# One core, windowed attention with a gated side branch: w_out goes to the head of the main load queue, w_in behind it

## The chip, the cores and the metric

The kernel runs on one core of a Trainium2 chip. A core has five engines that run side by side: TensorE (PE, matrix products), VectorE (DVE), ScalarE (ACT), GpSimd (POOL) and SyncE (SP), and 16 DMA engines that bring data from the chip's main memory into the on-chip memory of 128 partitions. In this kernel SP does little but issue loads; all loads that it issues stand in one queue. The metric is the device time of one execution in microseconds (us); lower is better. All data are 32-bit floats.

## The reference

Two sequences (B = 2), one new token each, width D = 512. The token's row is normalised, and goes two ways. One is attention over the last 4096 positions of a cache of 32768, with 32 query heads that share 8 key and value heads (4 to 1) of 128 numbers each. The other is a small gated network whose result, through SiLU, multiplies what attention gives.

```
xn = layernorm(x)                                    # (2, 1, 512)

# attention
q = xn @ wq                                          # wq (512, 4096): 32 heads of 128
k, v = last 4096 positions of the caches             # 8 heads, each used by 4 query heads
p = softmax(q k^T / sqrt(128))
s = (p v) @ wo                                       # wo (4096, 512)

# gate
z  = gelu(xn @ w_in)                                 # w_in (512, 1792)
z1, z2 = two halves of z (896 each);  z2 = layernorm(z2)
h  = z1 * (w_sp * z2 + b_sp)                         # w_sp, b_sp: one number each, as there is one token
g  = silu(h @ w_out)                                 # w_out (896, 512)

out = x + s * g
```

Most bytes are the keys and values: 2 x 2 x 8 x 4096 x 128 numbers, 67 MB. wq and wo have 8.4 MB each, w_in 3.67 MB and w_out 1.84 MB.

## The kernel before, in words

**Buffers.** Big loads land in a pool `ring` of four slots (up to 32 KB in each partition), which are used again in turn: `win` takes the first, `wq0` and `wq2` (two loads into its halves) the next two, the first keys `k0` the fourth; `k1` takes win's slot when the matmuls on win are through, `v0` that of `wq0`, `k2` that of `wq2`, `v1` that of `k0`, and so on. A second pool, `kts`, has two buffers. They hold `wout` and `z` first, then `qs` and `qx` (the queries on their way into another layout), then the transposed keys. The vector engine's transpose into `qx` waits for the matmuls that read `wout`, since `qx` takes its buffer.

**Order.** Every instruction of TensorE, VectorE, ScalarE and SP keeps the order in which the program is written (the class `InOrder`, so that nearly every instruction has the line 65 in the profile). Each engine works through its own list and waits at an instruction until its operands and buffers are ready. SP's list is: `win`, `wout`, three loads for w_q, then the keys and values in pairs of heads (eight units of 4.19 MB of keys and as much of values), and wo last. Completions of DMAs are counted on a few lanes that are used in turn; a load that takes a lane again waits until the lane's load before it has landed. The first load on SP's list and the first load of keys have the same lane.

**Front of the kernel (lines 118 to 339).** While `win` comes in, x is normalised and turned into columns (`xnT`), and constant tables are made. Then TensorE has, in this order: `z` (xn times w_in, in four pieces; ScalarE and VectorE copy the results out), `zT` (28 small matmuls that turn z into columns), `queries(0)`, a mean, `queries(1)`, a variance, `queries(2)`, `queries(3)` (16 matmul instructions each, on the four row blocks of w_q), and `y`, the product of the gate's hidden row `hT` with `wout`. VectorE and ScalarE work on GELU, the second layer norm and `hT` at the same time. `hT` is made from zT, the mean and the variance. Behind y come `qx` (transposed queries), `xm`, the matmul `qa`, and `y_sum`.

**The units (ORDER, line 27).** A string lists the steps of the attention part in the order in which they are issued. For unit 0 the list starts with the loads `K:0 K:1 V:0`, then `T:0.0` (the first of eight transposes of the unit's keys on VectorE, `kts<-k`), `q:0` (VectorE places the queries, `qb`), more transposes, and then `shares` and `scores` (TensorE), row maxima, exponentials (ScalarE, `p`), their transposes (`pT`), and `pv` (TensorE, `acc`, 16 instructions each for two halves). Later units have the same steps, one unit interleaved with the next. At the end come the products with wo (`part`, `so`), the sum with x and the store.

Of the kernel before, what the change touches and what calls it, by code (L numbers as in the profile page):

```python
# [9 lines left out]
F32 = mybir.dt.float32  # L10
# [4 lines left out]
P = 128  # L15
# [55 lines left out]
def kernel(  # L71
# [14 lines left out]
    pe, dve, act, sp = (InOrder(tc, e) for e in (nc.tensor, nc.vector, nc.scalar, nc.sync))  # L86
    B, _, D = x.shape
# [9 lines left out]
    FT = FH // P  # L97
# [8 lines left out]
    kts = ctx.enter_context(tc.tile_pool(name="kts", bufs=2))  # L106
# [4 lines left out]
    def slot(name, *shape):  # L111
        return ring.tile([P, *shape], F32, tag="slot", name=name)
# [5 lines left out]
    xs = sb.tile([B, D], F32, tag="ss", name="xs", bufs=1)  # L118
    act.dma_start(xs, x[:, 0, :])
    win_v = w_in.rearrange("(p k) f -> p k f", p=P)  # L120
    win = slot("win", KT, F)
    sp.dma_start(win, win_v)
    wout = kts.tile([P, FT, D], F32, tag="kts", name="wout")
    sp.dma_start(wout, w_out.rearrange("(p j) d -> p j d", p=P))
    wq_v = wq.rearrange("(p k) f -> p k f", p=P)
    wqt = []
    for a in range(0, KT, 2):
# [475 lines left out]
    for u in range(NU):  # L603
        p = Unit()
        p.u, p.m, p.kt, p.sh, p.ss, p.s, p.p, p.pT = u, None, {}, {}, {}, {}, {}, {}
        units.append(p)
    for line in ORDER.strip().split("\n"):
        for name in line.split():
            name, at = name.split(":")
# [35 lines left out]
```

## Time and profile before

| what | value |
|---|---|
| time, median of 3 runs | 216.86 us (216.77 to 216.94) |
| the profiled execution's own time | 217.29 us |
| its span, first to last instruction | 215.5 us |
| outside the span | 1.79 us |
| mean granted TensorE clock | 0.825 of full |
| busy: TensorE, VectorE, ScalarE, GpSimd | 143.2, 126.7, 51.6, 4.5 us |
| read from memory | 89.40 MB, 415 GB/s over the span |

The views used further on are these. The page's rows by slices cut the span into 40 equal parts and give tenths. A view by stage gives, for a stretch of time, the busy time of each engine with the number of its instructions, the granted clock, the mean busy share of the 16 DMA engines and the rate. A share slightly over 1 comes from packets that are counted where they begin. A timeline row gives the start, the length, the engine, the operation with its tiles, and in brackets how long the engine was idle before and what ended that. The chain that ended last goes back from the last instruction to whatever released each step. The list of DMA issues gives the size in KB and the time from issue to landing. PE is TensorE, PEld its loading of weights, SPq the queue of instructions that SP issues. A tile's view gives its instructions with least, median and greatest length in nanoseconds, and first and last start.

### The profile page before, as it was taken

Reading aid. Unit: us, or ns where it says so; the run is one execution under the profiler, and the core shown is the slowest. Engines: PE = TensorE matmul, PEld = TensorE weight load, DVE = VectorE, ACT = ScalarE, POOL = GpSimd, SP = SyncE. Lnnn points to the kernel's source line nnn. Section 1 sums busy time; section 2 is a strip of 40 time slices with the busy share of each in tenths; the row PEclk is TensorE's granted clock in tenths of the full one; section 3 lists DMA queues with packets and bytes.
Section 4 is the critical chain, followed back from the end, with each engine's and each line's share of the span. In section 5 each row is a group of like instructions: output and inputs, shape, how many; then the busy total and the mean of one; then the engine's idle time right before and its main releaser. Section 6 shows DMA issues by size and latency. Waiting matters only on the chain.

```text
span 215.5 us, 2332 instructions
## 1 busy us (share of the span) xinstructions
PE 143.2 (66%) x900; PEld 48.1 (22%) x900; DVE 126.7 (59%) x218; ACT 51.6 (24%) x129; POOL 4.5 (2%) x17
## 2 busy tenths in 40 slices
PE   0179796833854966964991795389259917987793
PEld 0117622111120221222220231123112201232231
DVE  2611213169899799649928972993698099636011
ACT  5011103300116036033330602142051206142201
POOL 8000000000000000000000000000000000000000
PEclk9999569665998896796697599669755997996999
DMA  7999999999999999999999999999999999999990
GB/s 246 432 443 444 398 429 465 414 458 414 456 408 447 420 426 444 426 443 426 450 420 450 408 441 420 426 450 426 447 415 456 401 456 414 447 426 417 420 374 22
DMA packets 3930, 89.54 MB, mean 416 GB/s; under 512 B 446, under 2 KB 462, under 8 KB 848
## 3 DMA queue, kind: packets, MB, share of 16 engines
q1 hardware_dynamic: 3900, 89.40, 96.8%
q8 instruction: 7, 0.11, 0.2%
q14 instruction: 3, 0.02, 0.0%
q10 hardware_dynamic: 20, 0.01, 0.0%
HBM read 89.40 MB, written 0.00 MB: 415 GB/s over the span
## 4 chain that ended last, share of the span: by engine, by line
DMA 63%; PE 23%; DVE 8%; ACT 3%; issue 1%; ACTq 0%
DMA v<-in_A_v_cache_dram 42%; DMA k<-in_A_k_cache_dram 16%; PE acc L65 10%; DMA win<-in_B_w_in_dram 5%; PE sh L65 5%; DVE kts L65 4%; PE part L65 4%; PE s L65 3%; DVE pT L65 1%; ACT p L65 1%; ACT o L65 1%; DVE gate L65 1%; PE mo L65 1%; ACT ss L65 1%; DVE qb L65 1%
## 5 line engine op out<-in xcount | busy, mean ns | idle before, releaser
L65 DVE STREAM_TRANSPOSE kts<-k 128x1024 f32<-128x1024 f32 x64 | 75.6, 1218 | 29.5 <-DMA k<-in_A_k_cache_dram 29.5
L65 PE MATMUL sh<-kts,qb 128*32 128x512 f32 x256 | 41.6, 775 | 13.2 <-DVE kts L65 9.3
L65 PE MATMUL acc<-v,pT 128*32 128x512 f32 x256 | 37.4, 707 | 8.8 <-DVE pT L65 4.4
L65 ACT ACTIVATE p<-s,nb 128x512 f32<-128x512 f32 x32 | 22.5, 733 | 36.2 <-DVE nb L65 36.2
L65 ACT ACTIVATE ss<-sh 128x512 f32<-128x512 f32 x16 | 9.6, 599 | 59.1 <-PE sh L65 59.1
L65 DVE STREAM_TRANSPOSE pT<-p 128x1024 f32<-128x1024 f32 x16 | 19.6, 1225 | 2.3 <-ACT p L65 2.1
L65 PE MATMUL s<-ss,sums 128*128 128x512 f32 x32 | 18.8, 671 | 2.3 <-ACT ss L65 2.3
L65 PE MATMUL mo<-mg,joint 128*128 128x16 f32 x16 | 4.0, 327 | 23.4 <-DVE mg L65 23.4
L65 PEld LDWEIGHTS acc<-v,pT 128*32 128x32 f32 x256 | 10.5, 145 | 35.1 <-issue 27.0
L65 PEld LDWEIGHTS sh<-kts,qb 128*32 128x32 f32 x256 | 8.8, 126 | 34.2 <-issue 28.8
L65 DVE TENSOR_REDUCE m<-s 128x1 f32<-128x512 f32 x16 | 10.7, 671 | 4.2 <-PE s L65 4.2
L65 PE MATMUL q_ps<-wq,xnT 128*32 128x512 f32 x64 | 10.5, 784 | 3.5 <-DMA wq<-in_A_wq_dram 3.5
L65 ACT ACTIVATE o<-acc,wd 128x128 f32<-128x128 f32 x32 | 9.1, 368 | 15.0 <-PE acc L65 15.0
L65 PEld LDWEIGHTS mo<-mg,joint 128*128 128x128 f32 x16 | 3.2, 250 | 27.2 <-DVE mg L65 24.4
L65 PE MATMUL z<-win,xnT 128*32 128x448 f32 x32 | 5.6, 869 | 4.7 <-DMA win<-in_B_w_in_dram 4.7
L65 PE MATMUL part<-wo,oT 128*32 128x512 f32 x56 | 7.7, 596 | 1.4 <-ACT o L65 1.4
L65 PEld LDWEIGHTS s<-ss,sums 128*128 128x128 f32 x32 | 5.0, 197 | 10.3 <-issue 7.7
L65 PE MATMUL zT_ps<-rowm,z 128*128 128x2 f32 x28 | 6.6, 370 | 0.0
L65 PEld LDWEIGHTS zT_ps<-rowm,z 128*128 128x128 f32 x28 | 6.5, 325 | 0.0
L65 ACT ACTIVATION_READ_ACCUMULATOR p<-s,nb 128x1 f32 x32 | 6.5, 203 | 0.0
L65 ACT ACT_TABLE_LOAD x4 | 5.1, 1283 | 2.6 <-POOL hT L164 2.6
L65 DVE COPY z<-z 128x448 f32<-128x448 f32 x2 | 1.3, 626 | 7.5 <-PE z L65 7.5
(111 smaller groups left out, 68.4 us busy)
## 6 DMA issues: line engine op xcount, KB each, us to landing
k<-in_A_k_cache_dram SPq DMA_DIRECT2D x8, 4096.0 KB, 27.4
v<-in_A_v_cache_dram SPq DMA_DIRECT2D x8, 4096.0 KB, 29.8
wq<-in_A_wq_dram SPq DMA_DIRECT2D x1, 4096.0 KB, 24.5
wq<-in_A_wq_dram SPq DMA_DIRECT2D x2, 2048.0 KB
wo<-in_A_wo_dram SPq DMA_DIRECT2D x1, 4096.0 KB, 30.4
win<-in_B_w_in_dram SPq DMA_DIRECT2D x1, 3584.0 KB, 11.5
wo<-in_A_wo_dram SPq DMA_DIRECT2D x1, 2048.0 KB
wout<-in_B_w_out_dram SPq DMA_DIRECT2D x1, 1792.0 KB, 15.3
```

Of the source, the lines that this page charges most:

```text
L65: return self.tc.keep_in_program_order(call(*args, **kwargs))
```

## The change

The two tiles are made and the two loads are issued in the other order. The pools are different (`ring` and `kts`), and each pool sees its own tiles in the same order as before, so that every tile keeps its place. On TensorE, VectorE, ScalarE and GpSimd the lists of instructions stay as they are. On SP the first two entries change places, and with them the lanes: the one that the first load of keys uses again belongs to `wout` afterwards, and to `win` before.

```
     win_v = w_in.rearrange("(p k) f -> p k f", p=P)
+    wout = kts.tile([P, FT, D], F32, tag="kts", name="wout")
+    sp.dma_start(wout, w_out.rearrange("(p j) d -> p j d", p=P))
     win = slot("win", KT, F)
     sp.dma_start(win, win_v)
-    wout = kts.tile([P, FT, D], F32, tag="kts", name="wout")
-    sp.dma_start(wout, w_out.rearrange("(p j) d -> p j d", p=P))
     wq_v = wq.rearrange("(p k) f -> p k f", p=P)
```

## The prediction

> **What bounds the kernel now.** I read the page first (span, DMA row, clock row, queues), then DMA share and rate by stage, then the timeline of the first 50 us by engine, then the chain that ended last and the last output-weight loads. The page's rows: the DMA row gives the mean busy share of the 16 DMA engines in 40 slices of 5.4 us, the PEclk row the granted TensorE clock in the same slices.
>
> ```profile
> span 215.5 us, 2332 instructions
> ...
> PEclk9999569665998896796697599669755997996999
> DMA  7999999999999999999999999999999999999990
> ...
> q1 hardware_dynamic: 3900, 89.40, 96.8%
> ```
>
> The main queue's DMAs (q1) carry 89.40 MB and keep the DMA engines busy for 96.8% of the span. By stage (window, its length, busy time of PE, PEld, DVE, ACT, POOL, and at the end of each row granted clock, DMA share, GB/s):
>
> ```profile
> 0.00:2.00 2.00, 0.00 (x0) 0.00 (x0) 0.35 (x2) 0.00 (x0) 1.45 (x12) 1.00 0.82 203
> 2.00:4.00 2.00, 0.00 (x0) 0.00 (x0) 1.15 (x5) 1.42 (x2) 2.00 (x4) 1.00 0.58 229
> ...
> 14.00:44.00 30.00, 24.51 (x140) 11.08 (x131) 7.08 (x28) 6.08 (x10) 0.00 (x0) 0.77 1.01 435
> 44.00:200.00 156.00, 106.04 (x642) 32.00 (x646) 113.52 (x159) 40.87 (x110) 0.00 (x0) 0.80 1.00 432
> ...
> 209.00:212.00 3.00, 2.90 (x52) 1.24 (x48) 0.00 (x0) 0.60 (x1) 0.00 (x0) 1.00 0.36 137
> ```
>
> From 14 to 200 us the engines are full (share 1.01 and 1.00, 435 and 432 GB/s); at that rate 89.40 MB alone take about 206 us. There is a start-up loss in the first 4 us and a run-out after 209. Two views of the end of the kernel, the tile wo (which instruction, how often, durations, first and last start) and the chain that ended last (start, length, what):
>
> ```profile
> L65 SPq DMA_DIRECT2D wo<-in_A_wo_dram x6: 334/426/432, 171.6 to 186.0; - x6
> ...
> DMA to landing us min/median/max: 25.5/25.7/30.4
> ```
> ```profile
> 77.09 27.29 DMA v<-in_A_v_cache_dram
> ...
> 195.29 3.27 PE acc L65 x16
> ...
> 198.87 1.93 PE acc L65 x16
> ...
> 211.33 0.93 PE so L65 x24
> ```
>
> The last load of wo is issued at 186.0 and lands 25.5 later, at 211.5. The last output matmuls (so) run from 211.33 to 212.26 and use it. The chain names PE in those last microseconds, but stream and TensorE arrive together there. So the time is the length of one unbroken stream of loads plus a short tail. The question for this change is whether the stream starts later, gets a hole, or moves other bytes.
>
> **The change, step by step.** It removes and adds nothing: the same two loads, 3.67 MB (128 rows of 28,672 bytes) and 1.84 MB (128 rows of 14,336), both on SP's queue, swap places. Instruction order on PE, DVE, ACT and POOL is the same. SP, and how the two loads land now:
>
> ```profile
> 0.73 0.39 SPq L65 DMA_DIRECT2D win<-in_B_w_in_dram  x1
> ...
> 1.18 0.41 SPq L65 DMA_DIRECT2D wout<-in_B_w_out_dram  x1
> ...
> 12.23 6.27 SPq L65 DMA_DIRECT2D k<-in_A_k_cache_dram  x2
> ...
> 32.50 0.53 SPq L65 DMA_DIRECT2D v<-in_A_v_cache_dram  x1
> ...
> 39.53 0.54 SPq L65 DMA_DIRECT2D k<-in_A_k_cache_dram  x1
> ```
> ```profile
> win<-in_B_w_in_dram SPq DMA_DIRECT2D x1, 3584.0 KB, 11.5
> ...
> wout<-in_B_w_out_dram SPq DMA_DIRECT2D x1, 1792.0 KB, 15.3
> ```
>
> *Landing times.* win lands at 0.73 + 11.5 = 12.2, wout at 1.18 + 15.3 = 16.5. Whatever is second lands when both are in, so win moves to about 16.5: 4.3 us later. wout lands first: its share is 4.3 us of transfer, and the start-up is 11.5 - 2 x 4.3 = 2.9, so near 0.7 + 7.2 = 7.9, where nobody needs it yet. Everything behind the pair (w_q, K, V) has the same bytes ahead of it: 0.
>
> *SP's queue.* The wait ahead of the first K load is a completion lane that this load shares with the first load of the queue; the row of SP's waits shows it:
>
> ```profile
> SPq L65 <- DMA win<-in_B_w_in_dram: 8.8, 1, 8.8
> ```
>
> After the swap that lane belongs to wout, so K0 is issued near 7.9, not 12.23. It stands behind w_q in the queue either way: 0. K1 needs win's buffer back, which is when the z matmuls end, near 18.0 now (the second issue, half a microsecond long, at the end of the row of 6.27 us) and near 22.3 after. The queue ahead of it is not empty before K0 has landed, just before 46.17 (the first key transpose, below): 23 us of cover. V0 (32.50) and K2 (39.53) wait for the query matmuls, dealt with next.
>
> *The front chain.* This is the only work that really moves. PE, in order (start, length, what, idle before it):
>
> ```profile
> 12.35 5.56 PE L65 MATMUL z<-win,xnT 128*32 128x448 f32 x32 [4.73 <-DMA win<-in_B_w_in_dram]
> ...
> 18.15 6.60 PE L65 MATMUL zT_ps<-rowm,z 128*128 128x2 f32 x28
> 26.18 3.64 PE L65 MATMUL q_ps<-wq,xnT 128*32 128x512 f32 x16 [1.43 <-DMA wq<-in_A_wq_dram]
> ...
> 30.29 2.14 PE L65 MATMUL q_ps<-wq,xnT 128*32 128x512 f32 x16
> 32.36 0.39 PE L65 MATMUL var_ps<-u,ones 128*128 128x14 f32 x2
> 32.68 1.92 PE L65 MATMUL q_ps<-wq,xnT 128*32 128x512 f32 x16
> 36.69 2.79 PE L65 MATMUL q_ps<-wq,xnT 128*32 128x512 f32 x16 [2.09 <-DMA wq<-in_A_wq_dram]
> 39.24 2.79 PE L65 MATMUL y<-wout,hT 128*32 128x512 f32 x14
> 44.27 1.12 PE L65 MATMUL qa<-xm,same 128*128 128x256 f32 x2 [2.25 <-DVE xm L65]
> ```
> ```profile
> 36.28 0.18 DVE L65 TENSOR_TENSOR hT<-zT 128x14 f32<-128x14 f32 x1
> ...
> 42.15 1.30 DVE L65 STREAM_TRANSPOSE qx<-qs 128x512 f32<-128x512 f32 x2 [5.68 <-PE y L65]
> ...
> 46.17 1.25 DVE L65 STREAM_TRANSPOSE kts<-k 128x1024 f32<-128x1024 f32 x1 [2.05 <-DMA k<-in_A_k_cache_dram]
> 47.34 1.19 DVE L65 TENSOR_TENSOR qb<-qa,grpm 128x1024 f32<-128x1024 f32 x1
> ```
>
> z starts near 16.65 and zT ends at 24.75 + 4.3 = 29.05. The first query group then finds its weights landed and loses its idle 1.43, so it starts at 29.05, 2.87 late. From there to the end of the third group PE runs without a break, 26.18 to 34.60, which now ends at 37.47. The fourth group, which waits 2.09 for w_q until 36.69 today, starts at 37.47: only 0.78 late. hT (36.46 + 2.87 = 39.33) is ready before PE is through with that group, so y ends at 42.03 + 0.78 = 42.81. Behind y come qx, the matmul qa and the placed queries qb. The qa matmul would end at 45.39 + 0.78 = 46.17, and qb starts at 47.34 because DVE first waits for K0 (2.05 idle). Cover: about 1.95; cost 0.
>
> Bounds: the same 16 query matmuls took between 1.92 and 3.64. All slow: the second, third and fourth groups add 1.50, 1.72 and 0.85, and y ends 4.9 late, 2.9 beyond the cover. All fast: y ends earlier than now, gain hidden. I take 0.78, because it leaves each row its own length. Without the cover those 2.9 us, or the 0.78, would fall on unit 0 first. What is late next is its V buffer, and the next covers are DVE's waits for later K loads:
>
> ```profile
> 75.42 3.50 DVE L65 STREAM_TRANSPOSE kts<-k 128x1024 f32<-128x1024 f32 x3 [1.41 <-DMA k<-in_A_k_cache_dram]
> ...
> 94.75 3.50 DVE L65 STREAM_TRANSPOSE kts<-k 128x1024 f32<-128x1024 f32 x3 [3.89 <-DMA k<-in_A_k_cache_dram]
> ```
>
> 1.41 and 3.89 us, 5.3 together, take up either. Nor would the queue run dry: the V load issued at 77.09 lands 27.29 later, while its own 4.19 MB need 9.7 at 432 GB/s, so some 17 us of other loads stand ahead of it.
>
> The Trainium skill, "TensorE: Matmul & The Clock Gate", Part 1 (the HAM clock gate), says that TensorE runs at half clock after an idle window of some 3.4 us and gets the full clock back after a busy one, in windows that run free of the kernel. The PEclk row (5 and 6 in the fifth and sixth slices, around the tiny zT matmuls and the first query group) agrees. By that rule, with the idle 2.09 gone, y would more often be warm and the front chain would end no later than today; by the rows it ends 0.78 late. Under the cover both give 0.
>
> *Start-up.* The first rows of the stream are now half as long; no row here shows a start with such rows. In the first 4 us the queue moved 203 x 2 + 229 x 2 = 0.86 MB against 1.74 MB at 435 GB/s: 2.0 us lost, part of it before the first byte. If the loss is a fixed time, the price is 0. If the start is paced per row (0.86 MB is 30 rows of 28,672), half-length rows move 0.43 MB less in that time: +1.0. If the loss per first row goes with its length, half of about 1 us is gained: -0.5. I take 0, nearest to what the two windows show: both are slow, and the rate is full afterwards with whichever rows.
>
> *Sum:* 217.29 of the profiled execution (215.5 of span and 1.79 around it) + 0 = 217.3; on the median of the runs, 216.86, which is 0.43 lower, it gives 216.9.
>
> **Rivals.**
>
> *Row-paced start (slower).* Place: the first 4 us of the stream. Price 0.5 (only the first row of each engine: 16 x 14,336 bytes = 0.23 MB) to 1.0, hence 217.4 to 217.9. For it: the rate in 2 to 4 us is still half. Against: once running, the stream holds 435 GB/s through wout's short rows as well. It decides if 0.19 MB or more are missing by 4 us. 0.15.
>
> *Length-paced start (faster).* 216.86 - 0.5 = 216.4, by the same windows. It needs the first rows' delay to shrink with their length. 0.08.
>
> *The tail's clock.* The 16 pv matmuls at 195.29 took 3.27, the same 16 at 198.87 took 1.93. If the half-clock stretch falls elsewhere, the tail shrinks or grows by about 1.3: 215.6 or 218.2. Against the gain: the last wo lands at 211.5 whatever PE does. Against both: units start on K landings by then, which do not move. 0.02 faster, 0.04 slower. The page of the Trainium skill named above has those windows run free of the kernel, so that the stretch would not hang on this change; no trace here shows their start.
>
> *The front delay reaches the end (slower).* It needs the queue to run dry, that is 17 us of cover used up by 4.9 at most; it would add at most 2.9: 219.8. 0.02.
>
> *The swap does nothing at all to landings,* because both loads interleave on the engines: against it stand 12.2 and 16.5. The time is the same, so it is within the forecast.
>
> **How the numbers follow.** Forecast, no change beyond 0.2% (0.43 us, about what a measurement of this kernel can tell from none): 0.69. Faster 0.08 + 0.02 = 0.10, and 0.02 more for what I have not seen: 0.12. Slower 0.15 + 0.04 + 0.02 = 0.21, of which the lower edge of the row-paced start may still be within the bound: 0.19. Range: 216.4 (the gain at start-up) to 217.6 (the row-paced start up to its middle); outside are the upper half of that rival, the tail and the front delay.
>
> **What would show it.** win's landing near 15.8 us after its issue and z at 16.6 show the first step; K0's issue near 8 the second. PE without idle between the zT matmuls and y, and y's end between 41 and 44, show the chain; DVE's first key transpose still at 46.2 the cover; share and rate of 14:44 and 44:200 unchanged, the unbroken stream; wo's last landing at 211.5 the end. Wrong would be: a rate well off 864 KB in the first 4 us (a start-up rival), a first key transpose that no longer waits for K0 and later K waits that shrink (front delay), or a DMA share under 0.98 in 14:200 (a hole in the stream).

## The result and the profile after

The changed kernel took 217.19 us (median of 20 runs, 217.00 to 217.36), the kernel before 216.83 in the same session (20 runs, 216.60 to 217.08). The ratio is 1.0016, with a 95% interval of 1.0009 to 1.0023: 0.36 us more, inside the 0.2% of the forecast, but not nothing. The profiled execution of after took 217.18 us with a span of 215.4. That of before, 217.29 with 215.5, lies above all 20 later runs of its kernel. So the two profiles differ in the opposite direction to the medians, and the 0.36 us cannot be found by laying these two side by side.

What the change did to the order of things can be. These are the main queue's issues and the landing times in the kernel after:

```profile
0.73 0.38 SPq L65 DMA_DIRECT2D wout<-in_B_w_out_dram  x1
1.18 0.41 SPq L65 DMA_DIRECT2D win<-in_B_w_in_dram  x1
...
8.05 14.10 SPq L65 DMA_DIRECT2D k<-in_A_k_cache_dram  x2
34.92 0.54 SPq L65 DMA_DIRECT2D v<-in_A_v_cache_dram  x1
38.81 0.54 SPq L65 DMA_DIRECT2D k<-in_A_k_cache_dram  x1
```
```profile
win<-in_B_w_in_dram SPq DMA_DIRECT2D x1, 3584.0 KB, 15.3
...
wout<-in_B_w_out_dram SPq DMA_DIRECT2D x1, 1792.0 KB, 7.3
```

win lands at 1.18 + 15.3 = 16.5, exactly when wout landed before; wout at 8.0, and K0 is issued then. TensorE and VectorE in the front, and VectorE's later waits for keys, in the kernel after:

```profile
16.65 4.91 PE L65 MATMUL z<-win,xnT 128*32 128x448 f32 x32 [9.03 <-DMA win<-in_B_w_in_dram]
...
21.79 6.60 PE L65 MATMUL zT_ps<-rowm,z 128*128 128x2 f32 x28
28.32 3.64 PE L65 MATMUL q_ps<-wq,xnT 128*32 128x512 f32 x16
...
35.10 3.64 PE L65 MATMUL q_ps<-wq,xnT 128*32 128x512 f32 x32
39.14 1.92 PE L65 MATMUL y<-wout,hT 128*32 128x512 f32 x14 [0.40 <-DVE hT L65]
```
```profile
46.44 1.25 DVE L65 STREAM_TRANSPOSE kts<-k 128x1024 f32<-128x1024 f32 x1 [3.29 <-DMA k<-in_A_k_cache_dram]
...
95.12 3.50 DVE L65 STREAM_TRANSPOSE kts<-k 128x1024 f32<-128x1024 f32 x3 [3.83 <-DMA k<-in_A_k_cache_dram]
```

z starts 4.30 us later than before (12.35), but y is done at 41.06, 0.97 us earlier than before (42.03). VectorE now waits 3.29 us for K0 instead of 2.05. The front was shortened on its way: the last two query groups (32 instructions in 3.64) and y (1.92 instead of 2.79) ran at the higher clock, without the idle 2.09 that stood between the groups before (granted clock from 14 to 44 us: 0.88, against 0.77 before).

The stream, by stage, in the kernel after (the same columns as in the prediction), and one row of before that was not shown there:

```profile
0.00:2.00 2.00, 0.00 (x0) 0.00 (x0) 0.35 (x2) 0.00 (x0) 1.45 (x12) 1.00 0.39 81
2.00:4.00 2.00, 0.00 (x0) 0.00 (x0) 1.16 (x5) 1.43 (x2) 2.00 (x4) 1.00 0.73 244
4.00:14.00 10.00, 0.61 (x4) 0.55 (x4) 3.28 (x22) 1.54 (x3) 1.01 (x4) 1.00 1.02 438
14.00:44.00 30.00, 24.72 (x146) 11.64 (x146) 7.21 (x28) 6.08 (x10) 0.00 (x0) 0.88 1.01 434
44.00:200.00 156.00, 103.82 (x637) 31.67 (x640) 113.27 (x158) 40.83 (x110) 0.00 (x0) 0.80 1.00 432
```
```profile
4.00:14.00 10.00, 2.26 (x16) 1.19 (x20) 3.27 (x22) 1.55 (x3) 1.01 (x4) 1.00 0.96 412
```

There is no hole in it: share 1.01 and 1.00 as before. The first 4 us look worse (81 x 2 + 244 x 2 = 650 KB against 864), while by 14 us the changed kernel looks ahead (0.65 + 4.38 = 5.03 MB after, 0.86 + 4.12 = 4.98 before). Neither can be read that way. The view books a whole packet (one row of a load) where it begins, so what it shows depends on how long the rows are that are in flight at the window's edge: at 4 us they are short in the kernel after, at 14 us in the kernel before. With the bytes of each packet spread evenly over its time, the four profiles of the old order (before twice, and two experiments below) have 4.86 to 4.90 MB at 14 us and 11.78 to 11.82 at 30, the three of the changed kernel 4.80 to 4.83 and 11.72 to 11.75. On average 0.05 MB are missing, 0.12 us at 432 GB/s, and at 199 us the same 0.05 MB are still missing (84.69 to 84.72 against 84.63 to 84.67). So about a third of the 0.36 us is lost by the whole stream in its first 14 us.

### The profile page after: what moved, and what is told of

Same layout as the page of the kernel before. It is cut to its first block, busy times and chain, and to the rows that moved or that the text cites. A ratio compares the mean times of both kernels' runs of the same rounds, so it can differ in the third digit from the quotient of the medians.

```text
span 215.4 us, 2332 instructions
## 1 busy us (share of the span) xinstructions
PE 140.5 (65%) x900; PEld 47.9 (22%) x900; DVE 126.7 (59%) x218; ACT 51.6 (24%) x129; POOL 4.5 (2%) x17
## 4 chain that ended last, share of the span: by engine, by line
DMA 60%; PE 18%; DVE 16%; ACT 3%; issue 1%; ACTq 0%
DMA k<-in_A_k_cache_dram 42%; DMA wo<-in_A_wo_dram 15%; DVE kts L65 11%; PE sh L65 7%; PE acc L65 4%; PE part L65 4%; DMA wout<-in_B_w_out_dram 3%; PE s L65 3%; ACT p L65 2%; DVE pT L65 2%; DVE m L65 1%; ACT ss L65 1%; DVE gate L65 1%; DVE nb L65 1%; DVE qb L65 1%
## 5 line engine op out<-in xcount | busy, mean ns | idle before, releaser
L65 PE MATMUL sh<-kts,qb 128*32 128x512 f32 x256 | 42.2, 785 | 14.4 <-DVE kts L65 10.8
L65 PE MATMUL acc<-v,pT 128*32 128x512 f32 x256 | 36.0, 682 | 8.5 <-DVE pT L65 5.5
L65 ACT ACTIVATE o<-acc,wd 128x128 f32<-128x128 f32 x32 | 9.1, 367 | 16.4 <-PE acc L65 16.4
L65 PE MATMUL z<-win,xnT 128*32 128x448 f32 x32 | 4.9, 762 | 9.0 <-DMA win<-in_B_w_in_dram 9.0
L65 PE MATMUL q_ps<-wq,xnT 128*32 128x512 f32 x64 | 9.7, 746 | 0.0
L65 DVE COPY z<-z 128x448 f32<-128x448 f32 x2 | 1.2, 625 | 11.2 <-PE z L65 11.2
## 6 DMA issues: line engine op xcount, KB each, us to landing
win<-in_B_w_in_dram SPq DMA_DIRECT2D x1, 3584.0 KB, 15.3
```

Source lines behind the costliest of these rows:

```text
L65: return self.tc.keep_in_program_order(call(*args, **kwargs))
```

## The experiments

Three theories for the 0.36 us were set against one another. A: the start of the stream with short rows costs it. B: the later front chain costs it. C: the earlier issue of K0 costs it. All ratios are to the kernel before, timed beside each experiment. A ratio and its interval come from all the runs, not from the two medians, and the quotient of the medians can differ from it: by up to 0.0008, and by 0.0021 in the one experiment whose runs scatter widely.

**The change again, twice.** The same file as the change, in two more sessions, to see whether the small ratio stays.

> The changed kernel once more, beside the kernel before, to see whether the small difference is a property of the order or of one chip session. If it belongs to the order (any of the theories below): ratio about 1.0016 again, 0.2 to 0.5 us more. If it came from the session: 1.000 +- 0.0007.

Measured: 217.24 against 216.80, ratio 1.0015 (1.0006 to 1.0023).

> The changed kernel a third time, in one call with the three above. Ratio about 1.0015 if the difference belongs to the order on every chip; nearer 1.000 if it hangs on the chip, as the kernel before was 217.03 in the session of the second call and 216.80 in the first.

Measured: 217.33 against 217.07, ratio 1.0020 (1.0011 to 1.0028). The kernel before itself moves by up to 0.27 us from session to session (216.80, 216.83, 217.03, 217.07), so times from different sessions are not compared below, only ratios. The difference belongs to the kernel and not to a session. Both of these sessions ran on one chip, so whether it is the same on every chip, which the second expectation asks, is not answered.

**The kernel before, as an experiment.**

> The kernel before, submitted like an experiment, for a second profile of it and to see what the comparison gives for no change at all. All theories: ratio 1.000 within about 0.0008, 216.8 us. If the first profile of before (217.29) was a slow specimen, this one has the last engine of the first two loads finished earlier than 16.48 us: near 16.1, as in the run with the late z.

Measured: 217.05 against 217.03, ratio 1.0004 (0.9995 to 1.0013). Its profiled execution took 216.68 with a span of 214.9, so the first profile (217.29) was a slow specimen. The sign that was expected of it, the two first loads complete near 16.1 us instead of 16.48, did not come: w_out lands 15.2 us after its issue, at 16.4. What differs is told under the table below.

**A late z with the old order of loads.**

```
+    held = ps.tile([P, 512], F32, tag="mo", name="held")
+    pe.matmul(held[0:32, 0:2], xnT[:, 0, :], wout[:, 0, 0:2], start=True, stop=True)
     for n in range(G):
         pz = bank(f"z{n}", 512)[:, :FC]
```

> The order of loads stays as before (w_in first), and one tiny matmul that reads w_out is put ahead of z on TensorE, so that z starts at about 16.6 us as in the changed kernel, while first rows, lanes and the issue of the first keys (near 12.2 us) stay as before. It computes a product that nobody uses. Theory A (the start of the stream with short rows costs the 0.36 us): 216.8, ratio 1.000. Theory B (the later front chain costs it): about 217.2, ratio 1.0016. Theory C (the earlier issue of the first keys): 216.8.

Measured: 216.93 against 216.80, ratio 1.0002 (0.9993 to 1.0011). TensorE in this run:

```profile
16.23 0.18 PE L65 MATMUL held<-wout,xnT 128*32 128x2 f32 x1 [8.61 <-DMA wout<-in_B_w_out_dram]
...
22.53 6.60 PE L65 MATMUL zT_ps<-rowm,z 128*128 128x2 f32 x28
```

The zT matmuls start at 22.53, later than in the changed kernel (21.79), and the time stays that of before (0.0002 more, with an interval that ends below 1.0016). Theory B falls.

**K0 issued early with the old order of loads.** The small load of x4 on ScalarE's queue moves behind `place_queries()`; the keys then share a lane with the first load of x.

```
-    act.dma_start(x4[0 : P : P // (G * B), :], ...)      # line 139
         if name == "q":
             place_queries()
+            act.dma_start(x4[0 : P : P // (G * B), :], ...)
```

> The order of loads stays as before, with w_in first in long rows and z near 12.2 us. Only the small load of x4 on ScalarE's queue moves behind the first query step, which shifts the lanes, so that the first keys are issued near 3.5 us. Theory C (the early issue of the first keys costs the 0.36 us): 217.2, ratio 1.0016. Theory A (short rows at the start): 216.8, ratio 1.000.

Measured: 217.13 against 217.03, ratio 1.0003 (0.9995 to 1.0012). The row of its queue:

```profile
3.27 15.42 SPq L65 DMA_DIRECT2D k<-in_A_k_cache_dram  x2
```

K0 is issued at 3.27 us, and no cost follows that could be told from none. Theory C, which asked for 1.0016, is not supported.

**Short rows at the start, with the old order.** w_in in two, then in four loads of whole row blocks:

```
-    sp.dma_start(win, win_v)
+    for k in (0, 2):
+        sp.dma_start(win[:, k : k + 2], win_v[:, k : k + 2, :])
```

> The order of loads stays as before, but w_in is loaded in two halves of two row blocks each, so that the stream starts with rows of 14,336 bytes as in the changed kernel, while z still starts near 12.2 us. One DMA more moves the lanes: the first keys are issued near 8 us. Theory A (short first rows): 217.2, ratio 1.0016. Theory B (front chain): 216.8. Theory C (early issue of the first keys): 217.2.

Measured: 217.09 against 216.80, ratio 1.0009 (1.0000 to 1.0018).

```
-    sp.dma_start(win, win_v)
+    for k in range(KT):
+        sp.dma_start(win[:, k : k + 1], win_v[:, k : k + 1, :])
```

> The order of loads stays as before, but w_in comes in four loads of one row block each, so that the stream starts with rows of 7,168 bytes. Theory A in its strong form (the shorter the first rows, the later the slowest engine): 217.3 or more, ratio 1.002 or more, and the pair of first loads complete after 16.5 us. If the length of the first rows does not matter: 216.8 to 216.9.

Measured: 217.22 against 217.03, ratio 1.0004 (0.9996 to 1.0013). The halves go half the way that theory A asks for, with an interval that reaches from nothing to all of it. The quarters should have cost more and did not: their interval ends below 1.0016, though it holds a small cost as well as none (all their eleven runs lie at or above 217.03). The strong form of A, the shorter the rows the worse, falls. Neither run differs from the kernel before in the rows alone. With w_in in pieces z does not start near 12.2 us, as was expected, but at 8.2 (halves) and 7.9 (quarters), on the pieces that have landed.

**Half the partitions at a time.** Meant as the partner of the halves with long rows:

```
-    sp.dma_start(win, win_v)
+    for p in (0, P // 2):
+        sp.dma_start(win[p : p + P // 2], win_v[p : p + P // 2])
```

> As in the run with halves, but w_in is cut into partitions 0 to 63 and 64 to 127, so that rows stay 28,672 bytes long, with the same lanes and the first keys issued near 8 us. Against the halves this changes the row length only. Theory A (short first rows): 216.8, ratio 1.000. Theory B (front chain): 216.8. Theory C (early issue of the first keys, or one DMA more): 217.2.

Measured: 226.02, ratio 1.0423 (1.0409 to 1.0438), which no theory had. The stage from 4 to 14 us in this run, and the landing of its two loads:

```profile
4.00:14.00 10.00, 0.61 (x4) 0.55 (x4) 3.27 (x22) 1.58 (x3) 1.01 (x4) 1.00 1.04 215
```
```profile
win<-in_B_w_in_dram SPq DMA_DIRECT2D x2, 1792.0 KB, 15.6
```

The DMA engines are fully busy (1.04) and move 215 GB/s, half of what the same stage moves otherwise. w_in's 3.67 MB take 17.1 us at 215 GB/s and 8.5 at 432; the 8.6 us between them are most of the 9.2 lost. The Trainium skill, "SBUF — State Buffer", Door 1 (the DMA port swizzle), says that partitions 0 to 63 reach only 8 of the 16 ports, and gives some 218 GB/s for 8 of them; the measured 215 agrees. As a test of row length the run is void. As a test of something else it is the clearest of all: a delay of 8.6 us put into the stream's start comes out at the end whole, while some 4 us put ahead of z (the run with the late z) do not come out at all.

**A long load ahead of both.** w_q's first half (4.19 MB in rows of 32,768 bytes) is issued first, then w_in, w_out and the rest of w_q:

```
+    (first pass of the w_q loop: t = slot("wq0", ...); sp.dma_start(t, ...))
     win = slot("win", KT, F)
     sp.dma_start(win, win_v)
     wout = kts.tile([P, FT, D], F32, tag="kts", name="wout")
     sp.dma_start(wout, ...)
     (second pass of the w_q loop)
```

> w_q's first 4.19 MB, in rows of 32,768 bytes, go ahead of w_in and w_out. z starts near 21.9 us, 9.7 us later than before and 5.2 later than in the changed kernel, so that the front chain passes its cover (y would end near 46 to 48, the first key transpose 2 to 5 us late). Theory A: the start has long rows, and the queue hides the late front: 216.8, ratio 1.000. Theory B (a later front chain reaches the end): 217.5 or more.

Measured: 216.76 against 217.03, ratio 0.9988 (0.9979 to 0.9997).

> The order w_q's first half, w_in, w_out once more, beside the two variants of it in this call. Theory D (the time is set by the slowest DMA engine: its lag behind the fastest at the start, plus the instruction fetches that hit it): if the start is again narrow (0.3 us between the first and the last engine of the first load), ratio 0.998 to 1.000; if the start is spread over 1 us, 1.000 to 1.002. The earlier ratio was 0.9988.

Measured: 216.78 against 217.07, ratio 0.9989 (0.9981 to 0.9998). VectorE and TensorE in the first of the two:

```profile
21.38 5.70 PE L65 MATMUL z<-win,xnT 128*32 128x448 f32 x32 [13.75 <-DMA win<-in_B_w_in_dram]
...
47.54 1.24 DVE L65 STREAM_TRANSPOSE kts<-k 128x1024 f32<-128x1024 f32 x1
```

The first key transpose no longer waits for K0 (no bracket) and starts 1.4 us later than at 46.17 (2 to 5 were expected): here the front's cover is gone. The kernel is faster than both others all the same, by a little over 0.1% than before. So a front chain that is past its cover by 1.4 us costs nothing either, as the queue still has loads in it.

**The exchange of the change, behind the long load.** The same with w_out ahead of w_in:

```
     (first pass of the w_q loop)
+    wout = kts.tile(...);  sp.dma_start(wout, ...)
     win = slot("win", KT, F)
     sp.dma_start(win, win_v)
-    wout = kts.tile(...);  sp.dma_start(wout, ...)
```

> w_q's first half, then w_out, then w_in: the same exchange of w_in and w_out as in the change, but behind a long load, so that the stream starts with rows of 32,768 bytes. Theory A (the cost of the change sits in the first rows of the stream): the same as the run with w_in ahead of w_out, ratio 0.999 +- 0.001. Theory B or any cost of w_in coming behind w_out as such: slower than that run by 0.0015. The front chain is late by 4.3 us more, z near 25.7 us.

Measured: median 216.74, ratio 1.0006 (0.9984 to 1.0027). Eight of its twelve runs lie between 216.66 and 216.85, as without the exchange; the other four at 217.27, 218.01, 218.07 and 219.31, and they lift the ratio over 1 though the median lies below that of before (217.07). The profile is of the 219.31. Its chain where the queries are placed, its queue around 80 us, its loads of keys, and the stages there:

```profile
54.08 1.22 DVE qb L65
```
```profile
63.24 0.53 SPq L65 DMA_DIRECT2D v<-in_A_v_cache_dram  x1
80.80 0.54 SPq L65 DMA_DIRECT2D k<-in_A_k_cache_dram  x1
```
```profile
DMA to landing us min/median/max: 15.2/26.6/33.4
```
```profile
80.00:84.00 4.00, 4.00 (x28) 1.12 (x24) 3.84 (x6) 0.00 (x0) 0.00 (x0) 0.88 0.98 377
84.00:92.00 8.00, 5.93 (x48) 1.93 (x40) 6.86 (x10) 4.23 (x12) 0.00 (x0) 1.00 0.97 406
```

The queries are placed at 54.08, 6.7 us later than in the kernel before (47.34). The load of keys at 80.80 is issued later in turn (71.88 before, 74.30 after), and the shortest time from issue to landing of a load of keys has fallen to 15.2 us, while its own transfer needs 9.7. In this execution the queue ran dry. The stream moved 377 x 4 + 406 x 8 = 4.76 MB between 80 and 92 us, where the kernel before moved 5.25; three DMA engines stood idle for 0.65 to 1.45 us at 83 us, and some packets behind took 2.5 to 3.2 us in place of 1.21. This is the rival of the front delay that reaches the end. It struck in this execution, with a front 6.7 us late; with w_q first and no exchange, where they are placed 1.6 us late (48.94), it did not. The other three long executions have no profile. In the eight short ones the exchange as such costs nothing, which speaks for a cost at the stream's start.

How much the front may be late is set by the load with the least ahead of it. These are the loads of keys, in the kernel before and in the kernel after:

```profile
DMA to landing us min/median/max: 22.8/27.4/33.9
```
```profile
DMA to landing us min/median/max: 20.8/26.7/38.4
```

The shortest is that of the load issued at 71.88 before and at 74.30 after. Its first packet began 11.2 us after the issue in this profile of before, 8.7 in the second one and 8.7 in the kernel after. In the run above, with the queue dry, it still took 2.3. So some 6 to 9 us of other loads stood ahead of it.

**The long load in two halves.** Rows of 16,384 instead of 32,768 bytes at the start; the rest as in the run with w_q first:

```
-        for k, n in ((0, 2),) if a == 0 else ((0, 1), (1, 1)):
+        for k, n in ((0, 1), (1, 1)):
```

> As the run with w_q first, but its first 4.19 MB are loaded in two loads of one row block each, with rows of 16,384 bytes. Only the row length (and one DMA more) differs. Theory A: slower than that run by 0.0015 (217.1 against 216.8). If the length of the first rows does not matter: the same.

Measured: 217.00 against 217.07, ratio 0.9998 (0.9989 to 1.0007), and 0.22 us more than its partner in the same session (216.78). A asked for 0.33. The intervals of the two ratios overlap, but ten of its eleven runs lie above 216.85, and nine of the partner's eleven at or below it, so a cost of the split is likely. It is not one of bytes: at 30 us both kernels have moved 11.86 MB (spread evenly as above), so the shorter rows did not slow the whole stream here.

**What the profiles of these runs have in common** (the half-partition loads are left out). The trace records every packet of the DMA engines, though not which engine had it. Packets can be linked, each to the one that ends where it starts, and this gives 16 chains, one for each engine. So one can note when the first and the last of the 16 engines finish the first load of the stream, and when the last one finishes the first, large load of wo near the end:

```
kernel                      first rows   first load done    last engine done   time of this
                            (bytes)      first .. last      with wo's first    execution
before                      28,672       10.80 .. 11.88     201.55             217.29
before, as an experiment    28,672       10.82 .. 11.78     200.99             216.68
late z                      28,672       10.97 .. 11.52     201.19             216.86
early K0                    28,672       10.94 .. 11.76     201.41             217.11
after                       14,336        6.57 ..  7.72     201.44             217.18
after, second               14,336        6.63 ..  7.68     201.56             217.33
after, third                14,336        6.66 ..  7.73     201.61             217.30
w_in in halves              14,336        6.63 ..  7.70     201.18             217.16
w_in in quarters             7,168        4.56 ..  5.11     201.02             217.04
w_q first                   32,768       12.11 .. 12.42     201.01             216.81
w_q first, again            32,768       11.96 .. 12.49     201.08             216.78
w_q first, in halves        16,384        7.18 ..  7.70     201.02             216.88
w_q first, exchanged        32,768       11.97 .. 12.57     203.62             219.31
```

The time of an execution is the last column but one plus 15.67 to 15.80 in ten of the thirteen (15.86 to 16.02 in the other three). So it is the slowest of the 16 DMA engines that sets the time. Its lag is made of two things. One is the spread at the start: 0.3 to 1.15 us between the first and the last engine, and an engine that is behind stays behind. The other is the loads of instructions (q8 in the page), one of which can be seen in this row of the kernel before, a window of 0.7 us:

```profile
q8 instruction: 1, 0.02, 8.6%
```

It is 16 KB, takes about 0.95 us, and the data packet behind it takes 1.7 instead of 1.2, so that its engine falls 1.4 us behind for good (1.41 to 1.43 in the five runs where one engine can be followed through the first of them). That hardly anything else changes the distances can be seen in the first profile of before. From a chain's end with w_in and w_out to its end with wo's first load it is 183.98 to 183.99 us in eight chains and 185.40 to 185.41 in six, and only two chains lie elsewhere (184.54 and 185.67).

If such a load hits an engine that started late, the end comes late. In that profile the engine that was last with w_in and w_out, at 16.14 us, was hit, and ended last, at 201.55. In the second profile of before the last one, at 16.05, was not hit; the one that ended last, at 201.00, had been through at 15.59. So the two profiles of the same kernel differ by which engine was hit.

The changed kernel had a spread of 1.05 to 1.15 in all three profiles, the old order with w_in whole 0.55 to 1.08 in four, the halves 1.07, the quarters 0.55, the runs with w_q first 0.3 to 0.6. These first loads differ in size, though. At a point that is the same for all, when w_in and w_out are both through, the last engine stands at 15.79, 16.02, 16.05 and 16.14 us in the old order with w_in whole, at 16.16, 16.20 and 16.21 in the changed kernel, at 16.23 with the halves and at 15.83 with the quarters. On average the changed kernel's last engine is 0.19 us later than that of the old order.

## Why the prediction was right, and what it missed

- *The bound.* Right: one unbroken stream, and a short tail behind it. More exactly it is the slowest of 16 streams, one for each engine, which the mean share (1.00) does not show.
- *Landing times and SP's queue.* Right to within 0.2 us: win 16.5 forecast and measured, z at 16.65, K0 issued at 8.05 (7.9 forecast).
- *The front chain.* Its cost of 0 was right, its size wrong: y came 0.97 us earlier, where 0.78 later was forecast. The step that failed is "leaves each row its own length": zT ended at 28.39 instead of 29.05, as z ran in 4.91 instead of 5.56, and then the fourth query group (about 1.8 instead of 2.79) and y (1.92 instead of 2.79) ran at the higher clock; the first group kept its 3.64, and the second was longer than before (2.42 against 2.14). What the prediction cited from the Trainium skill, "TensorE: Matmul & The Clock Gate", Part 1, that y would more often be warm once the idle 2.09 is gone, agrees with y's 1.92 (2.79 before). With the cover none of this mattered, and a little past it nothing was lost either, as the late z and both runs with w_q first show.
- *The queue's cover of some 17 us.* Enough for this change, but mis-sized. It was read from one V load (27.29 us to landing); the same rule gives 13.1 for the shortest load of keys (22.8 less 9.7), and its packets leave some 6 to 9. A front 6.7 us late was enough to empty the queue in the exchanged run, where the rival asked for 17. That did not decide here, since the front was not late at all.
- *Start-up.* This is the term that was mis-sized: 0 was put there, and all that is left of the 0.36 us points there. The exchange costs nothing behind a long load (eight of twelve runs), a late front costs nothing, an early K0 costs nothing that could be told from none. And the stream is behind by 0.05 MB, or 0.12 us, from its first 14 us to its end. The rival of the row-paced start had the right place and sign, but 0.5 to 1.0 us is too much: the whole stream lost 0.12, the kernel 0.36. Its mechanism is not confirmed, since the quarters cost no more than the halves and w_q's halved rows took nothing from the stream. The criterion for it, 864 KB in the first 4 us with 0.19 MB missing, was a bad one: the view shows 0.21 MB missing, of which some 0.04 are left on average when packets are spread evenly over their time.
- *The forecast.* That the time stayed within 0.2% is right for the reason given, the unbroken stream. That the start's price stayed inside the bound of 0.43 us was luck: no row in the prediction showed it.
- *What stays open.* That the slowest engine sets the time is shown by the table, and 0.12 us of lost stream by the bytes. In the seven profiles the last engine ended with wo's first load 0.25 us later in the changed kernel than in the old order (201.54 against 201.29 on average). Of these, 0.12 is the stream's own loss, 0.07 more is the last engine's larger lag when w_in and w_out are through, and the rest goes with which engine an instruction load hit. These sizes are only likely: three and four profiles do not settle a third of a microsecond. Why w_out's rows at the start cost the stream 0.12 us, and why the quarters started narrowly (0.55), is not known.

## What to carry to other kernels

Where one queue of loads is full from start to end, moving loads inside it moves only the work in front of their readers, and it is the queue's cover (time from issue to landing, less the transfer's own time) that tells how far that work may slip. Take it from the load that has least, not from a typical one. Look for what delays the stream itself, however early: the 8.6 us of the half-partition loads came out at the end whole. A count that books packets where they begin cannot compare loads with rows of different length over a few microseconds. And where a difference is below 0.2%, one profiled execution of each kernel can point the wrong way; look at how the profiled times lie in the spread of the runs first.

## What the runs showed of the hardware that was not expected

- Two loads into 64 partitions each, in place of one into 128, ran at 215 GB/s, where the same stage had 412 and 438 in the kernels before and after, with all DMA engines busy; a split that looked neutral cost 4.2%.
- An instruction load of 16 KB cost its DMA engine 1.4 us of a saturated stream, more than its own 0.95, and the engine never caught up.
- The 16 engines did not start alike: they finished the same first load up to 1.15 us apart, and engines that no instruction load hit kept their distance to 0.01 us over the next 184 us (eight engines in the first profile of before).
